# Attention, two MLPs and a Fourier stage in one kernel: a shorter conversion of doubles, and the state product in column halves

## The chip, the core and the metric

One NeuronCore of a Trainium2 chip runs the whole program in one launch. The metric is the device time of the launch in microseconds. Three timed executions of the kernel before gave 624.9, 626.17 and 627.99 us; the median is 626.17 us.

Engine names as in the profile: PE is the matrix engine (PEld its weight loads), DVE the VectorE, ACT the ScalarE, POOL the GpSimd, SP the queue from which nearly all transfers are issued.

## What is computed

Decayed linear attention over 2 batches and 8 heads, then a block that mixes tokens and channels, then a block with a two-dimensional Fourier transform, a normalisation and a channel MLP:

```python
for b in range(nb):                       # attention, block by block
    intra = einsum('bhic,bhjc->bhij', qb, kb) * Dmask
    intra = einsum('bhij,bhjd->bhid', intra, vb)
    inter = einsum('bhid,bhde->bhie', qb * lam_pow, kv_state)
    out[:, :, sl] = intra + inter
    kv_state = lam_block * kv_state + einsum('bhsd,bhse->bhde', kb * rev_pow, vb)
h = relu(xt @ w_tok1) @ w_tok2            # first block
u = x + h.transpose(0, 2, 1)
x = u + relu(u @ w_ch1) @ w_ch2
u = x + real(fft(fft(x, axis=1), axis=2)) # second block
out = u + relu(normalised(u) @ m_ch1) @ m_ch2
```

Sequence 768, head dimension 64, model dimension 512, hidden widths 256, 1536 and 2048, all results in float32. The weight matrices `w_tok1`, `w_tok2`, `w_ch1`, `w_ch2`, `m_ch1`, `m_ch2` reach the core as 64-bit floating point numbers, each read as two 32-bit words, and the core makes float32 of them itself.

## The kernel before, in words

**Attention** handles two heads at a time ("pairs", numbered 0 to 7, four for each batch), in six chunks of 128 positions. For each pair there are three steps. Scores (`s`, line 382): products of 64 rows, which DVE multiplies by the decay matrix (line 385). States (`u`, line 407): ACT first scales the keys (line 402), PE makes the chunk states, DVE chains them (lines 411 and 413). Result (`r`, `attention_out`, lines 417 to 434): ACT copies the states into a block-diagonal tile `bd` (line 424; first the states of two chunks, then of three), PE adds for each chunk the two heads' value products, each into its own 64 partitions (line 430), and from the second chunk on the state product (line 433), which takes both heads at once, 128 columns wide; ACT copies the result out after each three chunks (line 434). So there are 8 x 6 x 2 = 96 value products and 8 x 5 = 40 state products. The profile has two records for each of these float32 products.

**The order** of PE and SP is written out by hand. The string `EARLY` names the steps up to about 90 us in the order in which PE takes them (`s3` scores of pair 3, `u3` its states, `r3` its result, `x`, `h`, `o` the token mixing, `w` 8 idle transposes, `c` a turn of conversion, `l` a load, `m` a turn of the MLP). The order of DVE, ACT and POOL is set by the scheduler of the language, from the program's dependencies and its own costs. Each engine takes its instructions strictly in the order found so.

**Conversion.** A tile of doubles is loaded into a buffer `raw` (three of them; SP, line 185, waits until one is free). ACT takes the upper words into a tile `m` (`stage_abs`, line 204). DVE makes the float32 from `m` and the raw words (`word_ops`, lines 223 to 227): clamp, shift left by 3 and mask, put in the top bits of the lower word, put in the top bits of the upper word. The last of these frees the raw buffer. Then ACT rounds the tile (line 253) and POOL makes the remainder (line 254), and PE uses both in three products (lines 117 to 119). There are 63 conversions: 7 of token weights (tiles `m_t`), 56 of channel weights (`m_a`, `m_b`), 51 of them before 260 us and 12 between 440 and 540 us. In between weights come back from a scratch memory as float32.

**The rest**: from 90 us on PE runs the channel MLPs, with relu on ACT (line 486) and the remainder on DVE (line 487), the Fourier stage beside the MLP (260 to 440 us), and the last MLP in a form with seven instead of eight products (from 440 us on).

Of the kernel before, what the change touches and what calls it, by code (L numbers as in the profile page):

```python
# [14 lines left out]
AF = mybir.ActivationFunctionType  # L15
ALU = mybir.AluOpType
# [3 lines left out]
B, H, S, D = 2, 8, 768, 64  # L20
# [27 lines left out]
AHEAD = (10, 35)  # L48
BUFS = {"raw": 3, "man": 3, "hid": 4, "half": 5, "t": 9}

HI_LEAST = float(np.array(0x38000000, np.uint32).view(np.float32))
HI_MOST = float(np.array(0x47EFFFFF, np.uint32).view(np.float32))


def f32(ap):
    return ap.bitcast(F32)
# [3 lines left out]
def body(ctx: ExitStack, tc: tile.TileContext, qkv, kT, lam, w_tok1, w_tok2,  # L60
         w_ch1, w_ch2, m_ch1, m_ch2, dft, dft_x, out, scratch, singles):
    nc = tc.nc
# [14 lines left out]
    ts = nc.vector.tensor_scalar  # L77
    stt = nc.vector.scalar_tensor_tensor
# [61 lines left out]
    def width(key):  # L140
        return HS if key[0] == "t2" else 512
# [46 lines left out]
    def words(job):  # L188
        w = raws[job][:, :2 * width(job[1])].rearrange("p (n t) -> p n t", t=2)
        return w[:, :, 0], w[:, :, 1]  # L190

    def stage_abs():

        if at_["abs"] >= at_["load"]:
            return
        job = jobs[at_["abs"]]
        kind, key = job
        at_["abs"] += 1
        if kind in ("single", "sums"):
            return  # L200
        m = raw_p.tile([P, 512], U32, tag="man", name="m_" + "_".join(map(str, key)), bufs=BUFS["man"])[:, :width(key)]
        mans[job] = m
        with tc.issue_after(on_act["out", 1]):
            nc.scalar.activation(f32(m), f32(words(job)[1]), AF.Abs)  # L204

    def word_ops():


        job = jobs[at_["word"]]
        at_["word"] += 1  # L210
        if job[0] == "single":
            return []
        if job[0] == "sums":

            a11, a12, a21, a22 = (raws[job].bitcast(F32)[:, i * 256:(i + 1) * 256] for i in range(4))
            return [lambda: tt(out=a22, in0=a21, in1=a22, op=ALU.add),
                    lambda: tt(out=a21, in0=a11, in1=a21, op=ALU.subtract),
                    lambda: tt(out=a11, in0=a22, in1=a11, op=ALU.subtract),
                    lambda: tt(out=a12, in0=a12, in1=a11, op=ALU.subtract)]
        lo, hi = words(job)  # L220
        m = mans[job]
        del raws[job]
        return [lambda: ts(out=f32(m), in0=f32(m), scalar1=HI_LEAST, scalar2=HI_MOST, op0=ALU.max, op1=ALU.min),
                lambda: ts(out=m, in0=m, scalar1=3, scalar2=0x3FFFFFFF, op0=ALU.logical_shift_left,
                           op1=ALU.bitwise_and),
                lambda: stt(out=m, in0=lo, scalar=29, in1=m, op0=ALU.logical_shift_right, op1=ALU.bitwise_or),  # L226
                lambda: stt(out=m, in0=hi, scalar=0xC0000000, in1=m, op0=ALU.bitwise_and, op1=ALU.bitwise_or)]

    def stage_part():

# [30 lines left out]
    def convert(n=1, among=()):  # L261

        among = list(among)
        for _ in range(n):
            if at_["part"] < at_["word"] and (jobs[at_["part"]][0] == "ahead" or room(jobs[at_["part"]][1])):
                stage_part()
            if at_["word"] < at_["abs"] and at_["word"] < at_["part"] + 1:
                for op in word_ops():
                    op()
                    if among:  # L270
                        among.pop(0)()
            while at_["load"] < at_["word"] + BUFS["raw"] and len(raws) < BUFS["raw"] and load_next():
                pass
            if at_["abs"] < at_["word"] + 1:
                stage_abs()
        for op in among:
            op()
# [139 lines left out]
    def attention_out(b, hp, bd, bank):  # L417
        n = f"{b}_{hp}"
        t, sts, state = pair.pop((b, hp))
        v, qs = (t[:, i, :].rearrange("p (c j) -> p c j", j=C) for i in (2, 3))  # L420
        for cs in (slice(0, 2), slice(2, NC - 1)):
            for a in range(2):
                r = slice(a * D, (a + 1) * D)
                on_act["state", NP * b + hp] = nc.scalar.activation(bd[r, cs, r], state[r, cs, :], AF.Copy).ins
        for g in range(2):
            po = bank(f"po_{n}_{g}")
            for c in range(3 * g, 3 * g + 3):
                cs = slice((c - 3 * g) * C, (c - 3 * g + 1) * C)
                for a in range(2):
                    nc.tensor.matmul(po[a * D:(a + 1) * D, cs], v[:, c, a * D:(a + 1) * D],  # L430
                                     sts[c, a], start=True, stop=(c == 0), skip_group_check=True)
                if c > 0:
                    nc.tensor.matmul(po[:, cs], bd[:, c - 1, :], qs[:, c, :], start=False, stop=True, skip_group_check=True)
            on_act["out", NP * b + hp] = nc.scalar.activation(xT[b][:, hp, g * HS:(g + 1) * HS], po[:, :HS], AF.Copy).ins


# [532 lines left out]
    with tc.manual_schedule(engines={ENG.SP, ENG.PE}):  # L969
# [20 lines left out]
        def result(n):  # L990
            attention_out(n // NP, n % NP, bds[n % 2], x_bank if n == 7 else acc_bank)
# [155 lines left out]
```

## Time and profile before

| | us |
|---|---|
| timed executions, median (lowest to highest) | 626.17 (624.9 to 627.99) |
| the profiled execution, span of the core | 630.9 |
| PE busy in it | 605.1 (96%) |
| DVE busy | 459.5 (73%) |
| ACT busy | 236.2 (37%) |
| POOL busy | 145.2 (23%) |
| mean granted clock of PE | 0.985 |

Of the profiled execution only the span is given, not a time of its own by the clock of the timed ones. Its span is 4.7 us above the median of the timed executions. The busy time of an engine is the union of its records; a record of PE reaches to the modelled end of a product, so records overlap and the pace of PE is read from the starts.

### The profile page before, as it was taken

How to read it: one execution, taken by the hardware profiler on the slowest of the kernel's cores; microseconds unless marked ns; L12 is line 12 of the kernel's file. 1: busy time of each engine (PE TensorE's matmuls, PEld its weight loads, DVE VectorE, ACT ScalarE, POOL GpSimd, SP SyncE). 2: the span in 40 equal slices, each digit the busy share in tenths (PEclk: the TensorE clock that was granted, in tenths of full speed). 3: DMA queues.
4: the chain of work that ended last, by engine and by line, in shares of the span. 5: the costliest groups of instructions: out<-in, count | busy, mean ns of one | idle time of the engine just before them, and what ended most of it. 6: DMA issues, size and time to landing. Idle time of an engine off the chain costs nothing. (4 is left out here: it accounts for less than half of the span.)

```text
span 630.9 us, 9533 instructions
## 1 busy us (share of the span) xinstructions
PE 605.1 (96%) x3624; PEld 552.5 (88%) x3624; DVE 459.5 (73%) x886; ACT 236.2 (37%) x480; POOL 145.2 (23%) x119
## 2 busy tenths in 40 slices
PE   8899899989989999999999999999899998999997
PEld 7677689989988999999999999888799897889986
DVE  6698689999598838947696885785697798353535
ACT  2566454543233333233544451333353342311110
POOL 5153222312230040110262410024412242300000
PEclk9999799999999999999999999999999999999999
DMA  7953423425257727400032101002303524000005
GB/s 287 406 211 116 175 68 101 139 67 189 97 166 218 246 87 234 151 1 1 26 93 84 24 12 35 17 1 84 101 33 116 168 67 134 2 0 1 0 1 199
DMA packets 24637, 65.57 MB, mean 104 GB/s; under 512 B 2824, under 2 KB 3984, under 8 KB 24592
## 3 DMA queue, kind: packets, MB, share of 16 engines
q1 hardware_dynamic: 24304, 64.83, 30.8%
q8 instruction: 28, 0.46, 0.3%
q14 instruction: 17, 0.14, 0.1%
q10 hardware_dynamic: 288, 0.14, 0.1%
HBM read 54.99 MB, written 9.97 MB: 103 GB/s over the span
## 5 line engine op out<-in xcount | busy, mean ns | idle before, releaser
L119 PE MATMUL ac<-w_b,hid 128*128 128x512 f32 x192 | 75.9, 395 | 0.3 <-DVE hid L487 0.3
L118 PE MATMUL ac<-w_b,hid 128*128 128x512 f32 x192 | 75.7, 394 | 0.0
L117 PE MATMUL ac<-w_b,hid 128*128 128x512 f32 x192 | 74.9, 390 | 0.0
L487 DVE SCALAR_TENSOR_TENSOR hid<-ph,hid 128x384 fp32r<-128x384 f32 x68 | 37.6, 553 | 42.3 <-ACT hid L486 42.3
L118 PE MATMUL ac<-hid,w_b 128*128 128x384 f32 x192 | 65.0, 338 | 2.5 <-DVE hid L487 2.3
L117 PE MATMUL ac<-hid,w_b 128*128 128x384 f32 x192 | 64.8, 338 | 2.1 <-DVE xT L495 1.8
L119 PE MATMUL ph<-uh,w_a 128*128 128x384 f32 x192 | 64.3, 335 | 0.5 <-POOL w_a L254 0.5
L117 PE MATMUL ph<-uh,w_a 128*128 128x384 f32 x192 | 64.6, 337 | 0.0
L119 PE MATMUL ac<-hid,w_b 128*128 128x384 f32 x192 | 64.3, 335 | 0.0
L118 PE MATMUL ph<-uh,w_a 128*128 128x384 f32 x192 | 64.2, 334 | 0.0
L486 ACT ACTIVATE hid<-ph 128x384 fp32r<-128x384 f32 x68 | 33.0, 486 | 73.1 <-PE ph L119 72.9
L254 POOL TENSOR_TENSOR w_a<-m_a,w_a 128x512 fp32r<-128x512 f32 x18 | 25.8, 1434 | 105.2 <-ACT w_a L253 103.9
L119 PEld LDWEIGHTS ac<-w_b,hid 128*128 128x128 f32 x192 | 36.0, 188 | 8.5 <-DVE hid L487 0.8
L118 PEld LDWEIGHTS ac<-w_b,hid 128*128 128x128 f32 x192 | 36.0, 188 | 6.1
L117 PEld LDWEIGHTS ac<-w_b,hid 128*128 128x128 f32 x192 | 36.1, 188 | 5.8
L254 POOL TENSOR_TENSOR w_b<-m_b,w_b 128x512 fp32r<-128x512 f32 x18 | 25.6, 1420 | 67.7 <-ACT w_b L253 38.2
L118 PEld LDWEIGHTS ac<-hid,w_b 128*128 128x128 f32 x192 | 36.1, 188 | 4.5 <-DVE hid L487 4.5
L117 PEld LDWEIGHTS ac<-hid,w_b 128*128 128x128 f32 x192 | 36.1, 188 | 3.1 <-ACT m_b L204 1.3
L119 PEld LDWEIGHTS ph<-uh,w_a 128*128 128x128 f32 x192 | 36.0, 188 | 0.8 <-POOL w_a L254 0.8
L118 PEld LDWEIGHTS ph<-uh,w_a 128*128 128x128 f32 x192 | 36.1, 188 | 0.1
L117 PEld LDWEIGHTS ph<-uh,w_a 128*128 128x128 f32 x192 | 36.1, 188 | 0.1
L119 PEld LDWEIGHTS ac<-hid,w_b 128*128 128x128 f32 x192 | 36.1, 188 | 0.0
(456 smaller groups left out, 1499.9 us busy)
## 6 DMA issues: line engine op xcount, KB each, us to landing
qkv<-qkv SPq DMA_DIRECT2D x7, 768.0 KB, 8.4
single_scratch<-m_a SPq DMA_DIRECT2D x16, 256.0 KB, 4.2
qkv<-qkv SPq DMA_DIRECT2D x10, 384.0 KB, 5.7
kp<-kT SPq DMA_DIRECT2D x8, 384.0 KB, 6.6
out<-u SPq DMA_DIRECT2D x11, 256.0 KB, 2.0
single_scratch<-m_b SPq DMA_DIRECT2D x10, 256.0 KB, 4.3
raw_t_0d<-w_tok SPq DMA_DIRECT2D x2, 384.0 KB, 7.0
raw_t_1d<-w_tok SPq DMA_DIRECT2D x2, 384.0 KB, 3.2
```

What stands on the lines that cost most here:

```text
L117: nc.tensor.matmul(ps, wt[0], xt[0], start=first, stop=False, **kw)
L118: nc.tensor.matmul(ps, wt[0], xt[1], start=False, stop=False, **kw)
L119: nc.tensor.matmul(ps, wt[1], xt[0], start=False, stop=last, **kw)
L254: nc.gpsimd.tensor_tensor(out=t[:, 1, :n], in0=src, in1=f32(t[:, 0, :n]), op=ALU.subtract)
L486: nc.scalar.activation(hi, ps, AF.Relu)
L487: stt(out=lo, in0=ps, scalar=0.0, in1=f32(hi), op0=ALU.max, op1=ALU.subtract)
```

## The change

The clamp of the upper word is gone, so a conversion takes three DVE operations. ACT multiplies the upper words by 2 to the power -112 where it took their absolute value; DVE then shifts left by 3 (without a mask), puts in the lower word's bits, and puts in the sign (one bit where it was two). In attention the state product is issued once for each head, 64 columns wide, where it was issued once for both. Between lines 54 and 223 a line of the kernel before has a number one higher in the changed kernel, between lines 225 and 433 one lower, and from line 434 on the same.

```diff
-HI_LEAST = float(np.array(0x38000000, np.uint32).view(np.float32))
-HI_MOST = float(np.array(0x47EFFFFF, np.uint32).view(np.float32))
+DOWN = 2.0 ** -112
...
-            nc.scalar.activation(f32(m), f32(words(job)[1]), AF.Abs)
+            nc.scalar.activation(f32(m), f32(words(job)[1]), AF.Copy, scale=DOWN)
...
-        return [lambda: ts(out=f32(m), in0=f32(m), scalar1=HI_LEAST, scalar2=HI_MOST, op0=ALU.max, op1=ALU.min),
-                lambda: ts(out=m, in0=m, scalar1=3, scalar2=0x3FFFFFFF, op0=ALU.logical_shift_left,
-                           op1=ALU.bitwise_and),
+        return [lambda: ts(out=m, in0=m, scalar1=3, scalar2=None, op0=ALU.logical_shift_left),
                 lambda: stt(out=m, in0=lo, scalar=29, in1=m, op0=ALU.logical_shift_right, op1=ALU.bitwise_or),
-                lambda: stt(out=m, in0=hi, scalar=0xC0000000, in1=m, op0=ALU.bitwise_and, op1=ALU.bitwise_or)]
+                lambda: stt(out=m, in0=hi, scalar=0x80000000, in1=m, op0=ALU.bitwise_and, op1=ALU.bitwise_or)]
...
-                if c > 0:
-                    nc.tensor.matmul(po[:, cs], bd[:, c - 1, :], qs[:, c, :], start=False, stop=True, skip_group_check=True)
+                for a in range(2 if c > 0 else 0):
+                    nc.tensor.matmul(po[a * D:(a + 1) * D, cs], bd[:, c - 1, a * D:(a + 1) * D],
+                                     qs[:, c, :], start=False, stop=True, skip_group_check=True)
```

The scheduler of the language moves instructions of DVE and ACT with it; PE and SP keep their order, except for the doubled product. Three places:

PE, the second and third chunk of pair 0's result (`po` is the accumulator, `att` holds `bd`), before:

```order
L433 MATMUL po_0_0_289<-qkv_0_105,att 128x128
L430 MATMUL po_0_0_289<-st_0_0_213,qkv_0_105 64x128
L430 MATMUL po_0_0_289<-st_0_1_215,qkv_0_105 64x128
L433 MATMUL po_0_0_289<-qkv_0_105,att 128x128
L430 MATMUL po_0_1_299<-st_0_0_213,qkv_0_105 64x128
```

and now:

```order
L432 MATMUL po_0_0_289<-qkv_0_105,att 64x128 x2
L429 MATMUL po_0_0_289<-st_0_0_213,qkv_0_105 64x128
L429 MATMUL po_0_0_289<-st_0_1_215,qkv_0_105 64x128
L432 MATMUL po_0_0_289<-qkv_0_105,att 64x128 x2
L429 MATMUL po_0_1_301<-st_0_0_213,qkv_0_105 64x128
```

Every product of the step now has the shape 64x128; nothing else moves on PE.

DVE, around the scores of pair 6 (`st`) and the conversion of the token weights (`m_t_0_0` first, then `m_t_1_0`; `x_1` is the token mixing's input), before:

```order
L223 TENSOR_SCALAR m_t_0_0_718<-m_t_0_0_718 128x384
L224 TENSOR_SCALAR m_t_0_0_718<-m_t_0_0_718 128x384
L385 TENSOR_TENSOR st_2_0_648<-s_2_0_0_638,att 128x512
L385 TENSOR_TENSOR st_2_1_650<-s_2_0_1_639,att 128x512
L385 TENSOR_TENSOR st_1_2_637<-s_2_1_0_652,att 128x256
L385 TENSOR_TENSOR st_1_2_637<-s_2_1_1_653,att 128x256
L113 TENSOR_TENSOR x_1_661<-px_3_662,x_1_661 128x512
L113 TENSOR_TENSOR x_1_661<-px_4_669,x_1_661 128x512
L113 TENSOR_TENSOR x_1_661<-px_5_676,x_1_661 128x512
L226 SCALAR_TENSOR_TENSOR m_t_0_0_718<-raw_t_0_0d,m_t_0_0_718 128x384
L223 TENSOR_SCALAR m_t_1_0_735<-m_t_1_0_735 128x384
L227 SCALAR_TENSOR_TENSOR m_t_0_0_718<-raw_t_0_0d,m_t_0_0_718 128x384
```

and now:

```order
L224 TENSOR_SCALAR m_t_0_0_740<-m_t_0_0_740 128x384
L225 SCALAR_TENSOR_TENSOR m_t_0_0_740<-raw_t_0_0d,m_t_0_0_740 128x384
L226 SCALAR_TENSOR_TENSOR m_t_0_0_740<-raw_t_0_0d,m_t_0_0_740 128x384
L224 TENSOR_SCALAR m_t_1_0_756<-m_t_1_0_756 128x384
L384 TENSOR_TENSOR st_2_0_673<-s_2_0_0_663,att 128x512
L384 TENSOR_TENSOR st_2_1_675<-s_2_0_1_664,att 128x512
L384 TENSOR_TENSOR st_1_2_662<-s_2_1_0_677,att 128x256
L384 TENSOR_TENSOR st_1_2_662<-s_2_1_1_678,att 128x256
L225 SCALAR_TENSOR_TENSOR m_t_1_0_756<-raw_t_1_0d,m_t_1_0_756 128x384
L114 TENSOR_TENSOR x_1_686<-px_3_687,x_1_686 128x512
L114 TENSOR_TENSOR x_1_686<-px_4_694,x_1_686 128x512
L114 TENSOR_TENSOR x_1_686<-px_5_701,x_1_686 128x512
```

The last operation on `m_t_0_0`, which frees its raw buffer, has moved from behind seven operations on scores and inputs to before them.

ACT, around the states of pairs 6 and 7 (`qkv_3` is pair 7's tile, `state_2` pair 6's states, `xT` the results), before:

```order
L486 ACTIVATE h1s_1_0_802<-h_0_1_783 128x512
L253 ACTIVATE w_a_0_997<-m_a_0_984 128x512
L424 ACTIVATE att<-state_2_823 64x2x64
L402 ACTIVATE qkv_3_807<-qkv_3_807,att 128x5x64 x2
L424 ACTIVATE att<-state_2_823 64x2x64
L424 ACTIVATE att<-state_2_823 64x3x64 x2
L204 ACTIVATE m_b_0_995<-raw_b_0d 128x512
L204 ACTIVATE m_a_1_1006<-raw_a_1d 128x512
L434 ACTIVATE xT_178<-po_2_0_876 128x384
```

and now:

```order
L401 ACTIVATE qkv_3_832<-qkv_3_832,att 128x5x64
L486 ACTIVATE h1s_1_0_827<-h_0_1_808 128x512
L401 ACTIVATE qkv_3_832<-qkv_3_832,att 128x5x64
L205 ACTIVATE m_b_0_1027<-raw_b_0d 128x512
L423 ACTIVATE att<-state_2_848 64x2x64 x2
L205 ACTIVATE m_a_1_1037<-raw_a_1d 128x512
L423 ACTIVATE att<-state_2_848 64x3x64 x2
L205 ACTIVATE m_b_1_1062<-raw_b_1d 128x512
L434 ACTIVATE xT_178<-po_2_0_901 128x384
```

The first steps of three conversions (`m_b_0`, `m_a_1`, `m_b_1`) now stand ahead of pair 6's state copies and of its first result copy; before, two of them stood between these.

## Rows read from the trace of the kernel before

**Rows 1.** The page, engines: busy time, share of the span, instructions.
```profile
PE 605.1 (96%) x3624; PEld 552.5 (88%) x3624; DVE 459.5 (73%) x886; ACT 236.2 (37%) x480; POOL 145.2 (23%) x119
```

**Rows 2.** Stretches: length, busy PE, PEld, DVE, ACT, POOL, then PE's clock, DMA.
```profile
100.00:260.00 160.00, 153.10 (x851) 147.74 (x851) 130.85 (x231) 56.80 (x105) 32.88 (x24) 1.00 0.50 160
...
440.00:540.00 100.00, 95.33 (x465) 85.25 (x464) 82.43 (x150) 38.58 (x72) 29.17 (x20) 0.98 0.30 98
```

**Rows 3.** One stretch of PE alone: length, busy, clock, DMA share, GB/s.
```profile
69.80:80.00 10.20, 10.20 (x47) 0.50 0.15 53
```

**Rows 4.** Waits of PE's weight loads, whole span: us in total, times, longest.
```profile
PEld po L433 <- issue: 7.6, 39, 0.3
...
PEld ac L118 <- DVE hid L487: 4.5, 7, 1.6
PEld pc L117 <- DVE hid L487: 3.8, 2, 3.1
PEld ht L117 <- DVE xT L477: 2.5, 2, 1.8
```

**Rows 5.** Timeline of PE, result of pair 0: start us, length us, records.
```profile
12.19 0.66 PE L430 MATMUL po<-st,qkv 128*64 128x128 f32 x8
12.78 0.49 PE L433 MATMUL po<-qkv,att 128*128 128x128 f32 x2
13.20 0.44 PE L430 MATMUL po<-st,qkv 128*64 128x128 f32 x4
13.56 0.49 PE L433 MATMUL po<-qkv,att 128*128 128x128 f32 x2
13.98 0.44 PE L430 MATMUL po<-st,qkv 128*64 128x128 f32 x4
```

**Rows 6.** Weight loads of lines 430 and 433: ns least, median, most.
```profile
L430 PEld LDWEIGHTS po<-st,qkv x192: 132/136/231, 12.2 to 85.9; 128*64 128x64 f32 x192
...
L433 PEld LDWEIGHTS po<-qkv,att x80: 186/189/338, 12.8 to 86.3; 128*128 128x128 f32 x80
```

**Rows 7.** Timeline of PE, result of pair 6.
```profile
74.07 0.70 PE L430 MATMUL po<-st,qkv 128*64 128x128 f32 x4
...
75.42 0.70 PE L430 MATMUL po<-st,qkv 128*64 128x128 f32 x4
```

**Rows 8.** Timeline of PE: the states of pairs 2, 3 and 7.
```profile
19.77 1.19 PE L407 MATMUL u<-qkv 128*64 128x64 f32 x19 [0.82 <-ACT qkv L402]
...
28.20 1.12 PE L407 MATMUL u<-qkv 128*64 128x64 f32 x11 [1.63 <-ACT qkv L402]
...
68.64 1.19 PE L407 MATMUL u<-qkv 128*64 128x64 f32 x19 [1.85 <-ACT qkv L402]
```

**Rows 9.** Timeline of ACT: a conversion's first step, the keys of pair 4.
```profile
27.03 0.66 ACT L204 ACTIVATE m_t<-raw_t_0d 128x512 f32<-128x512 f32 x1 [1.48 <-DMA raw_t_0d<-w_tok]
...
33.48 1.01 ACT L402 ACTIVATE qkv<-qkv,att 128x320 f32<-128x320 f32 x2 [3.19 <-DMA qkv<-qkv]
```

**Rows 10.** Timeline of SP's transfer issues: two token weights; pair 7's keys and values.
```profile
41.72 14.41 SPq L185 DMA_DIRECT2D raw_t_1d<-w_tok  x2
...
58.87 0.43 SPq L362 DMA_DIRECT2D qkv<-qkv  x1
```

**Rows 11.** Waits of SP's queue, whole span: total, times, longest.
```profile
SPq L185 <- DVE m_t L227: 20.1, 5, 13.6
```

**Rows 12.** Line 223 by stretch: length, DVE busy, clock, DMA share, GB/s.
```profile
100.00:260.00 160.00, 18.96 (x37) 1.00 0.50 160
440.00:540.00 100.00, 4.94 (x12) 0.98 0.30 98
```

**Rows 13.** The chain of waits, 444 to 456 us: start us, us, what.
```profile
445.51 3.19 DMA raw_a_10d<-m_ch
...
449.42 0.44 DVE m_a L223
```

**Rows 14.** ACT: line 204 in one conversion; a scaled copy of 256 columns (ns).
```profile
L204 ACT ACTIVATE m_a<-raw_a_0d x1: 671/671/671, 61.6 to 61.6; 128x512 f32<-128x512 f32 x1
...
L766 ACT ACTIVATE y_1s<-y x4: 400/412/423, 295.0 to 366.1; 128x257 f32<-128x257 f32 x2, 128x255 f32<-128x255 f32 x2
```

## The prediction

> **What bounds the kernel now.** I read the table of engines first: PE is busy for 605.1 of 630.9 us, DVE for 459.5, ACT for 236.2 [rows 1]. So the end comes earlier only where PE has less to do, waits less, or runs at a better clock; work taken from DVE or ACT counts through these alone. Then the stretches, for the change works in three of them. From 100 to 260 us PE is busy for 153.10 of 160 us and DVE for 130.85; from 440 to 540 us PE for 95.33 of 100, DVE for 82.43 [rows 2]. The first 90 us hold the attention, and there the clock is the third matter: from 69.8 to 80.0 us PE is never idle and runs at 0.50, its lower level of 1.2 GHz [rows 3]. The waits of the weight loads then tell for whom PE waits [rows 4]: for DVE's `hid` in the MLPs (4.5 us in seven waits, 3.8 in two), and 39 times, 7.6 us in all and never over 0.3, in front of line 433, the state product, with nothing but "issue" behind it. The timeline shows what that is [rows 5].
>
> **State product in halves, on PE.** A chunk of a pair's result takes 13.98 − 13.20 = 0.78 us: 13.56 − 13.20 = 0.36 from the first of its four value records to the state product, then 13.98 − 13.56 = 0.42 for the state product's two records [rows 5]. Without state products in between, PE does eight value records in 12.78 − 12.19 = 0.59 us [rows 5]; against four in 0.36, the other four took 0.23. After the change all products of a chunk have the shape of these: two heads' value products and two heads' state products, eight records, 2 x 0.23 = 0.46 us, 0.32 less a chunk. Bounds: no gain, if the halves cost the 0.42 that the wide product costs; at best 0.42 − 0.23 + (0.36 − 0.23) = 0.32. I take the upper end, since the wide product is the only one of another shape and the four records behind it are slow as well (0.36). Five such chunks a pair, eight pairs: 40 x 0.32 = 12.8 us of PE at full clock. At half clock a chunk takes 75.42 − 74.07 = 1.35 [rows 7], and should take 2 x 0.46 = 0.92.
>
> How much reaches the end goes by who holds PE next:
> - Pairs 0 and 1: nothing. The states of pairs 2 and 3 start at 19.77 and 28.20, after waits of 0.82 and 1.63 us for ACT's scaled keys [rows 8], and before that ACT had waited for a transfer (`raw_t_0d`, until 27.03) [rows 9]. What PE saves it waits longer.
> - Pairs 2 and 3: ACT gets pair 4's keys only at 33.48, from a transfer [rows 9]. Pair 2's result runs around that time, pair 3's after it. Of 2 x 1.6 (five chunks x 0.32) I take 1.4, bounds 0 and 3.2.
> - Pairs 4 and 5: nothing of the kind stands behind them; 2 x 1.6 = 3.2.
> - The states of pair 7 wait 1.85 us at 68.64 [rows 8]. The keys and values come late: SP was held at line 185 for a free raw buffer, 13.6 us at the longest [rows 11], between the issues that begin at 41.72 and last 14.41 [rows 10], and so issues pair 7's at 58.87 only. The buffer is freed by line 227 of `m_t_0_0`, which now stands ahead of pair 6's scores and the inputs of the mixing on DVE: seven operations earlier, and one operation of its own less. I expect SP free 4 to 5 us sooner. That covers the 1.4 + 3.2 = 4.6 us by which PE comes sooner, and takes some 0.8 off the 1.85 (bounds −4.6, which is the transfer landing as late as now, and +1.85).
> - Pair 6 runs at half clock: five chunks x (1.35 − 0.92) = 2.15. ACT has three conversions' first steps (671 ns each [rows 14]) among its state copies now, where it had two; I allow 0.35 for that and take 1.8.
> - The spell at half clock goes on to 80.0, some 3.6 us beyond pair 6, which costs 1.8. With a shorter wait ahead of it it may end sooner: half, 0.9, between 0 and the 5.1 that a spell of 10.2 us costs as a whole [rows 3].
> - Pair 7: 1.6.
>
> Attention in all: 1.4 + 3.2 + 0.8 + 1.8 + 0.9 + 1.6 = 9.7 us.
>
> **Three operations instead of four, on DVE.** Line 223 takes 18.96 us in 37 operations from 100 to 260 us, and 4.94 in 12 from 440 to 540 [rows 12]. All of it is taken from DVE. The other three operations keep their tiles and widths, only constants change: nothing. PE can get back no more than it idles there: 160 − 153.10 = 6.9 us and 100 − 95.33 = 4.7 [rows 2]. In the first stretch the waits that I see are for `hid`, which DVE makes between conversions [rows 4]; with 18.96 us less ahead of it, most of them should go: 4 of 6.9, bounds 0 and 6.9. In the second the longest wait is one of 3.1 us [rows 4], at the end of a chain of a transfer of 3.19 us, ACT and line 223's 0.44 [rows 13]. Of that chain only the 0.44 goes, and the DVE work queued ahead; but a PE that idles less also loses less clock, 0.98 being the mean there [rows 2], which is 2 us of 100. I take 3 of 4.7 + 2, bounds 0.4 and 5. From 260 to 440 us nothing is converted: 0.
>
> **The scaled upper words, on ACT.** Line 204 reads every second word of 128x512 and takes 671 ns; a copy with a scale takes 412 for 257 columns [rows 14]. Per column that is 1.3 and 1.6 ns, so a scaled conversion of 512 could take 0.82 at worst; 63 x 0.15 = 9.5 us of an engine that is busy 37% of the span [rows 1]. I take no change, as the fixed part of a 257-column operation is shared by fewer columns; the cover is ACT's idle time. At the worst price it would show in attention, where three such steps stand ahead of pair 6's copy: 0.45 us.
>
> **The sum.** 9.7 + 4.0 + 3.0 = 16.7, so the profiled span goes from 630.9 to 614.2. It stands 4.7 above the median of the timed executions, about one spell of half clock. If the timed ones don't have that spell, the 0.8 and 0.9 and part of pair 6's gain are not there (some 2.7 us): 626.2 − 14.0 = 612.2; if they do, 609.5. I say 611; by the bounds of the large terms 605 to 616.
>
> **Rivals.**
> - *Transfers and ACT hold the attention.* The gain of pairs 2 to 5 is eaten by a longer wait for pair 7's keys (−4.6 in the bound above), and PE is at half clock behind it as before. Left: 1.8 + 1.6 + 7 = 10.4, less some of the DVE term: 616 to 619. For it: every early step waits for transfers [rows 8, 9]. Against: the freed buffer [rows 11].
> - *DVE's relief brings nothing.* PE is busy 96% in both stretches, and behind DVE may come ACT's rounding or the transfer of the chain [rows 13]. Then only attention counts: 9.7 less 0 to 1, 617.
> - *Slower: the halves' weight loads aren't hidden.* The 64-column load takes 136 ns in line 430, the 128-column one 189 [rows 6]. The change has four loads and four records of products a chunk where it had two and two. If each load had to wait for the product before it, four of 0.136 and four products of about 0.115 (0.23 / 2) make 1.0 us instead of 0.42: 40 x 0.58 = +23, of which the waits of pairs 0 and 1 hide about 4, and DVE's 7 come off: 638. It turns the sign once a chunk's state product costs some 0.2 us more than now. Against it: in the first chunk four loads of 136 ns, 0.54 in all, fit into 0.23 us for four records [rows 5, 6], so loads do run beside other loads or products where the halves alternate. The Trainium skill, "TensorE: Matmul & The Clock Gate", Part 3, Packing small matmuls, says that a weight load overlaps running products only when it goes to other row groups; here all products have the same 128 rows, so by it this rival would hold. The rows disagree.
> - *The scaled copy is no cheaper way:* at 0.15 us more each it delays what DVE waits for, and takes back a part of the 7 us of DVE's term: 614 to 616, inside the forecast.
>
> **How the numbers follow.** Forecast 0.62; attention held by transfers 0.18; DVE's relief empty 0.14; weight loads not hidden 0.03; 0.03 for what I don't see. The low end, 602, has the whole of attention's 12.8, the 5.1 of clock and most of both DVE bounds; the high end, 620, has both of the first two rivals in part. A measurement of this kernel can tell about 0.5%, 3.1 us: faster is below 623.0, slower above 629.3. Both of the first two rivals are still faster; only both at full together come to the middle: same 0.06. Slower 0.04.
>
> **What would show it.** Right: after the change a chunk of pair 0's result takes 0.46 us from one value product to the next chunk's, and the waits of line 432 named "issue" are gone; pair 7's keys and values are issued before 55 us, and its states wait under 1.2 us; PE's idle time is near 3 us from 100 to 260, and DVE's busy time there down by 19. Wrong: a chunk above 0.7 us (the halves aren't packed); a wait of over 4 us ahead of pair 7's states; DVE down by 19 and PE's idle time still 7 (PE waits for others there); line 205 above 0.75 us. A time above 620 needs at least two of these, and one above 629 the third rival.

## The result: 1.2% faster, about half of what was forecast

The changed kernel took 619.68 us (median of four executions, 618.34 to 622.71) against 626.75 for the kernel before: a ratio of 0.9876 with the interval 0.9844 to 0.9908, so 7.1 us less. A later comparison, six executions against fourteen, gave 619.14 against 627.76, ratio 0.9862 (0.9825 to 0.9900). The forecast was 611, 15 us less, with 620 as its upper end: the sign was right, the gain forecast was twice what came, and the bounds of the large terms, 605 to 616, do not hold it.

The engines and the stretches of the changed kernel's profile, whose span is 617.2 us, answer to [rows 1 to 3]:

```profile
PE 589.6 (96%) x3704; PEld 545.2 (88%) x3704; DVE 438.3 (71%) x823; ACT 235.0 (38%) x480; POOL 144.4 (23%) x119
```

```profile
69.80:80.00 10.20, 10.20 (x88) 9.59 (x87) 10.20 (x20) 6.27 (x14) 2.88 (x3) 1.00 0.31 102
100.00:260.00 160.00, 155.58 (x872) 150.47 (x871) 112.25 (x194) 53.69 (x101) 30.09 (x21) 1.00 0.48 152
440.00:540.00 100.00, 96.01 (x477) 85.93 (x477) 77.83 (x136) 37.33 (x70) 27.71 (x20) 1.00 0.29 90
```

PE is busy 15.5 us less, by the halves and by the three stretches of half clock in the profile before, some 17 us in all, that are missing. From 100 to 260 us DVE has 18.6 us less to do, and PE's idle time there has fallen from 6.9 to 4.4 us; from 440 to 540 from 4.7 to 4.0. No stretch at half clock is left in this execution.

The second and third chunk of pair 0's result, to be held against [rows 5], and the loads of the halves, against [rows 6]:

```profile
12.84 0.39 PE L429 MATMUL po<-st,qkv 128*64 128x128 f32 x4
13.06 0.39 PE L432 MATMUL po<-qkv,att 128*64 128x128 f32 x4
13.28 0.39 PE L429 MATMUL po<-st,qkv 128*64 128x128 f32 x4
```

```profile
L432 PEld LDWEIGHTS po<-qkv,att x160: 132/137/137, 12.6 to 74.8; 128*64 128x64 f32 x160
```

A chunk takes 13.28 − 12.84 = 0.44 us instead of 0.78. The eight loads of a chunk, 8 x 0.137 = 1.1 us, lie within these 0.44. So the halves do on PE what was forecast (0.46), 40 x 0.34 = 13.6 us in all. Record by record, the trace shows the two heads' products starting 0.007 us apart, and such a pair every 0.11 us; of the whole product the second record started 0.21 us after the first. Why the wide records come so slowly no run isolates: that they were the only ones of another shape, as the prediction had it, is not tested.

Three groups of PE's waits, as [rows 4], and below them the waits inside the later pairs, from PE's timeline:

```profile
PEld u L406 <- ACT qkv L401: 6.2, 9, 2.0
PEld ac L119 <- DVE hid L487: 5.5, 9, 1.1
...
PEld po L432 <- ACT att L423: 1.9, 4, 1.0
```

```profile
33.93 0.56 PE L432 MATMUL po<-qkv,att 128*64 128x128 f32 x3 [1.72 <-ACT att L423]
...
35.59 0.71 PE L432 MATMUL po<-qkv,att 128*64 128x128 f32 x3 [0.34 <-ACT att L423]
...
39.78 0.44 PE L449 MATMUL px<-ident,xT 128*128 128x128 f32 x2 [0.89 <-ACT xT L434]
...
63.16 0.74 PE L406 MATMUL u<-qkv 128*64 128x64 f32 x17 [0.60 <-ACT qkv L401]
...
66.39 0.71 PE L432 MATMUL po<-qkv,att 128*64 128x128 f32 x3 [0.74 <-ACT att L423]
```

The 39 small stops called "issue" in front of the state product are gone (one entry of 1.9 us for line 432 still has that name among the waits of the loads; it is the stop at 33.93). In their place PE waits for ACT: for pair 3's state copies (1.72 and 0.34 us), for the copy of pair 3's result (0.89), for pair 6's state copies (0.74). The wait ahead of pair 7's states has fallen to 0.60 us [rows 8].

### The profile page after: what moved, and what is told of

It reads as the page before. It is cut to its first block, busy times and chain, and to the rows that moved or that the text cites. A ratio compares the mean times of both kernels' runs of the same rounds, so it can differ in the third digit from the quotient of the medians.

```text
span 617.2 us, 9630 instructions
## 1 busy us (share of the span) xinstructions
PE 589.6 (96%) x3704; PEld 545.2 (88%) x3704; DVE 438.3 (71%) x823; ACT 235.0 (38%) x480; POOL 144.4 (23%) x119
```

## The experiments

Every verdict is a ratio to the kernel before on the same chip; the medians of before in the three comparisons were 627.48, 627.92 and 627.76 us.

### What the kernel before does from one execution to the next

> The kernel before once more, for the clock and the span of each of its timed executions. Theory (the profiled execution of before was not a typical one: its three stretches at half clock cost some 8 us, and the timed executions mostly lack them): most executions have a mean granted clock of 0.99 or more and a span of 622 to 626 us, two us under their time; a new profile has less than 8 us of PE at 0.5. Rival (the stretches belong to the kernel, and its timed executions have them all): every execution shows a clock near 0.985 and a span near 631. Ratio 1.00 for both.

The kernel was not edited. Ratio 1.0026 (0.9993 to 1.0059), 627.94 us. The mean clock of its twelve executions lay between 0.988 and 0.997, their spans between 623.2 and 632.2 us; of 23 further ones two had a clock of 1.000 and spans of 621.9 and 623.3. The new profile has 625.5 us at a clock of 0.993, with two stretches of half clock, some 7 us. The theory holds in the main: eight of the twelve have a clock of 0.99 or more, though only six a span of 622 to 626 us. What the clock takes changes from one execution to the next, and the one that the prediction was worked from, with a clock of 0.985 and 630.9 us, is near the slow end of them. The time is some 1.8 us above the span throughout.

### One part at a time

The halves alone:

```diff
-                if c > 0:
-                    nc.tensor.matmul(po[:, cs], bd[:, c - 1, :], qs[:, c, :], start=False, stop=True, skip_group_check=True)
+                for a in range(2 if c > 0 else 0):
+                    nc.tensor.matmul(po[a * D:(a + 1) * D, cs], bd[:, c - 1, a * D:(a + 1) * D],
+                                     qs[:, c, :], start=False, stop=True, skip_group_check=True)
```

> The kernel before with the state product in halves and nothing else. Theory (most of the 7 us come from the halves: 40 chunks x 0.34 = 13.6 us of PE, of which some 9 go into waits for ACT and transfers): 4 to 6 us faster than before, 620.5 to 622.5. Rival (the halves alone gain next to nothing, since pair 7's keys come as late as before, and it is the freed raw buffer that lets the gain through): 0 to 2 us faster, and the wait ahead of pair 7's states grows to 4 us or more.

The shorter conversion alone (the changed kernel with the old state product; the diff above the other way round):

> The kernel before with the shorter conversion and nothing else. Theory (PE's waits behind 100 us come from single DVE operations in front of hid, of which few go): 1 to 3 us faster than before, 623.5 to 625.5, with DVE some 20 us less busy. Rival (the step that failed is the transfer of the gain in attention, and DVE's relief is worth the 7 us that were forecast): 5 to 8 us faster, 618.5 to 621.5.

The halves alone: 628.94 us, 1.0031 (1.0007 to 1.0055), no gain at all. The conversion alone: 619.37 us, 0.9875 (0.9845 to 0.9906), as much as the whole change. In both pairs the rival had the time. The first rival's reason did not come true, though: with the halves alone the wait ahead of pair 7's states is 2.29 us, not 4 or more (1.97 in the second trace of the kernel before), and pair 7's values are issued at 55.68 us (56.67 there).

The halves do arrive in attention. Where one and the same product starts was read from both traces, that of the kernel before at 625.5 us and that of the halves alone at 624.8: behind attention 86.39 against 81.25 us, 5.1 earlier with the halves; in the middle of the first MLP 128.91 against 126.81, 2.1 earlier; at its end 255.22 against 254.31, 0.9; the last one 0.6. The first of these products, before and with the halves:

```profile
86.39 0.34 PE L118 MATMUL ht<-w_t,h1s 128*128 128x384 f32 x1
```

```profile
81.25 0.34 PE L118 MATMUL ht<-w_t,h1s 128*128 128x384 f32 x1
```

The clock has a part in this: some 2 of the 5.1 are a stretch at half clock that only the first trace has in attention (0.98 up to 100 us), and 1.8 of what is given back is one that only the second has behind it (0.97 in the second row below). The rest, some 2.5 us, came back as idle time of PE: 8.9 us from 80 to 260 us, against 6.4 without the halves. The waits listed there grew from 3.9 to 5.4 us for DVE's `hid`, and from 0.8 to 3.1 for steps of ACT. These are single executions. Two of the changed kernel, at the same clock up to 450 us, lie 1.0 us apart behind attention and 1.8 at the end of the first MLP, so a smaller difference between traces carries little. The kernel with the halves alone, by stretch:

```profile
80.00:100.00 20.00, 19.43 (x116) 18.30 (x115) 19.90 (x33) 10.80 (x20) 7.10 (x5) 1.00 0.34 116
100.00:160.00 60.00, 57.01 (x307) 54.77 (x306) 51.59 (x89) 22.80 (x43) 13.44 (x10) 0.97 0.36 120
```

DVE is busy for 19.90 of 20 us where PE comes out of attention. It has the conversions of the MLP's weights to do there as well as the remainders that PE waits for. A full DVE alone does not show that PE waits for it: with the conversion alone it is as full in these 20 us, and PE is never idle.

```profile
80.00:100.00 20.00, 20.00 (x120) 19.30 (x119) 19.97 (x30) 11.10 (x21) 6.69 (x5) 1.00 0.36 117
```

That it is DVE that takes the gain is shown by the runs below, which change its work.

### Is it DVE's load, or the buffer that it frees earlier?

```diff
-                lambda: stt(out=m, in0=hi, scalar=0x80000000, in1=m, op0=ALU.bitwise_and, op1=ALU.bitwise_or)]
+                lambda: stt(out=m, in0=hi, scalar=0x80000000, in1=m, op0=ALU.bitwise_and, op1=ALU.bitwise_or),
+                lambda: ts(out=f32(m), in0=f32(m), scalar1=-3.0e38, scalar2=3.0e38, op0=ALU.max, op1=ALU.min)]
```

> The changed kernel with a fourth DVE operation a conversion, a clamp that changes nothing, put behind the one that frees the raw buffer. DVE has the load of before, the raw buffer is freed one operation earlier than before. Theory (the load is what counts): as the halves alone with the old conversion, 627 to 629.5, and PE waits for DVE behind 100 us as there. Rival (the earlier free buffer, hence the earlier transfers, is what counts): as the changed kernel, 619 to 621.

629.66 us, 1.0031 (1.0007 to 1.0055): the same as the halves with the old conversion, and 10 us above the changed kernel. Freeing the buffer one operation earlier, with DVE's load as before, brings nothing. It does not price an earlier transfer: pair 7's values are issued at 57.09 us in this trace, no earlier than in the kernel before (56.67). The trailing clamp also makes each conversion as long as before, not only DVE's load, and the scheduler orders DVE and ACT anew in every run here; no run holds these apart. That the load is what counts is read from the waits of PE. Those of its loads for a converted weight come to 1.2 us in all; the long ones are for what DVE makes besides (`hid` and `xT` for the MLPs, `u`, a sum in the last MLP) and, in attention, for ACT's keys:

```profile
PEld ac L119 <- DVE hid L488: 6.6, 7, 1.6
PEld u L407 <- ACT qkv L402: 5.5, 7, 2.2
PEld pb L118 <- DVE u L632: 4.7, 3, 3.3
PEld ht L118 <- DVE xT L478: 3.1, 4, 1.8
PEld pc L118 <- DVE hid L488: 3.0, 1, 3.0
```

Against the changed kernel's trace the same products start 2.8 us later behind attention (91.92 against 89.09), 5.8 at the end of the first MLP (264.24 against 258.41), 10.5 behind the last conversions (536.60 against 526.09). The clock has a large part: this trace has stretches of half clock from 19.4, 67.2 and 521.2 us, each 3.4 us long and so worth 1.7, that the changed kernel's has not. Without them nothing is left of the 2.8 beside attention, about 3 us are lost in the first MLP and about 3 behind 440 us. The next two runs take the places apart by the timed executions, with the trailing clamp in the conversions of one place only:

> The changed kernel once more, as the reference of the next three on one chip: 618.5 to 620.5 by every theory.

> The changed kernel with the trailing clamp in the twelve conversions behind 440 us alone. Theory (with the clamp in all conversions the trace fell back by 2.8 us up to 90 us, by 3.0 from there to 260, by 4.7 from 430 to 530; each stretch pays for its own operations): 3 to 5 us slower than the changed kernel, 622.5 to 624.5. Rival (the late loss came with the earlier ones, since the stretch was entered later): within 1 us of it.

> The changed kernel with the trailing clamp in the first sixteen conversions alone, those beside the attention. Theory (each stretch pays for its own): 2 to 3.5 us slower than the changed kernel, 621.5 to 623. Rival (what is lost in attention is got back behind it, where PE waits for DVE in any case): within 1 us of it.

```diff
+                lambda: ts(out=f32(m), in0=f32(m), scalar1=-3.0e38, scalar2=3.0e38, op0=ALU.max, op1=ALU.min)][:4 if job[0] == "double" and job[1][1] == 1 and job[1][0] in "ab" else 3]
```

(the late ones; for the early ones the condition is `at_["word"] <= 16`). The reference took 619.14 us (0.9862, 0.9825 to 0.9900); the late twelve 622.42 (0.9913, 0.9883 to 0.9944), 3.3 more; the first sixteen 621.84 (0.9906, 0.9869 to 0.9942), 2.7 more. Both are what the theory said, though the intervals overlap that of the reference. The first sixteen lie between 30 and 102 us of their trace. If the places add, some 4 of the 10 us are left for the 35 in between. Not all of this is waiting. With the product of span and mean clock taken as the span without the clock's losses, the means are 615.2 us (reference), 616.2 and 616.3: about 1 us each, within the scatter of the executions, and the rest goes with the mean clock, 0.9963 against 0.9927 and 0.9942.

### Still fewer operations

```diff
-                lambda: stt(out=m, in0=lo, scalar=29, in1=m, op0=ALU.logical_shift_right, op1=ALU.bitwise_or),
```

> The changed kernel without the operation that puts in the lower word's bits (the lowest three bits of each converted weight are left out): two DVE operations a conversion. Theory (DVE's load sets the pace behind the attention, so that what attention saves is given back there; the first operation taken away let it through, a second gives less): 2 to 4 us faster than the changed kernel, about 616. Rival (three operations are already off the path, PE's waits that are left are single operations in front of hid): within 1 us of the changed kernel, 619 to 620.5.

and without the shift as well:

> The changed kernel with one DVE operation a conversion, the sign (shift and lower word's bits left out, so the weights are wrong by a power of two and in their lowest bits). Theory (load): 1 to 2 us below the kernel with two operations, 614 to 615. Rival: as the changed kernel, 619 to 620.5.

Two operations: 615.43 us, 0.9797 (0.9763 to 0.9831), another 4 us. One: 616.91 us, 0.9823 (0.9793 to 0.9853), no further gain. The first of these kernels, by stretch:

```profile
80.00:100.00 20.00, 20.00 (x120) 19.19 (x119) 13.18 (x25) 10.15 (x20) 3.90 (x3) 1.00 0.40 135
100.00:160.00 60.00, 59.37 (x332) 57.39 (x331) 33.15 (x61) 21.31 (x41) 12.28 (x9) 1.00 0.27 92
```

With DVE at 46 of 80 us PE idles for 0.6 us in these, and little is left to relieve. But most of the 4 us are not won there, for the changed kernel idles for only 1.3 us in them. In the two traces the same products start within 0.2 us of each other at 440 us and 3.3 apart at 540, and from 440 to 540 us PE is busy for 98.55 us instead of 96.01. (Before that the trace with two operations loses 1.7 us by a stretch of half clock in attention, which the other has not.)

If that is the reason why the halves bring nothing, they should bring something here. So the state product was made whole again in the kernel with two operations (the first diff the other way round):

> The state product whole again, with two DVE operations a conversion (the lower word's bits left out, as in the run with two operations, which took 615.4 us with the halves). Theory (what the halves save in PE is given back to DVE as long as DVE has three or four operations; with two the halves pay): 3 to 5 us slower than with the halves, 618.5 to 620.5. Rival (the halves pay nothing whatever DVE does, because inside the attention ACT and transfers hold PE): 614.5 to 616.5.

618.66 us, 0.9847 (0.9812 to 0.9883), 3.2 us more than with the halves, as the theory had it; the two intervals overlap a little. In the two traces the halves are 3.6 us ahead behind attention (89.02 against 92.66) and still 2.8 at the end. All together, medians in us:

| DVE operations a conversion | state product whole | in halves |
|---|---|---|
| four | 626.8 to 627.9 | 628.9 (old conversion), 629.7 (trailing clamp) |
| three | 619.4 | 619.1 and 619.7 (the change) |
| two (lowest bits left out) | 618.7 | 615.4 |

### The waits for ACT inside attention

In the changed kernel ACT's timeline ahead of the waits at 33.93 and 35.59 us reads:

```profile
31.68 1.02 ACT L401 ACTIVATE qkv<-qkv,att 128x320 f32<-128x320 f32 x2 [3.12 <-DMA qkv<-qkv]
32.60 0.47 ACT L434 ACTIVATE xT<-po 128x384 f32<-128x384 f32 x1
32.97 0.61 ACT L252 ACTIVATE w_t<-m_t 128x512 fp32r<-128x512 f32 x1
33.49 0.62 ACT L423 ACTIVATE att<-state 64x128 f32<-64x128 f32 x2
```

Pair 4's keys, which wait for a transfer, stand ahead of pair 3's state copies. They were put behind them:

```diff
-        behind = (("table", 0), ("state", 0), ("out", 0), ("out", 1))[min(NP * b + hp, 3)]
+        behind = (("table", 0), ("state", 0), ("out", 0), ("out", 1), ("state", 3))[min(NP * b + hp, 4)]
```

> The changed kernel with one order on ACT altered: the scaling of pair 4's keys, which waits for a transfer, comes behind the copies of pair 3's states instead of ahead of them. Theory (the waits of 1.7 and 0.3 us of PE in pair 3's result, at 33.9 and 35.6 us of the changed kernel's trace, are this order's, and what they cost reaches the end): 1.5 to 2.5 us faster than the changed kernel, 617 to 618.5. Rival (the next wait takes it: the copies of pair 3's result, pair 5's keys or the inputs of the mixing come no earlier): within 0.7 us of the changed kernel, 619 to 620.5, and the waits stand a little later, in front of the mixing's inputs.

and in a second kernel the rounding of the first token weights too:

```diff
-        nc.scalar.activation(t[:, 0, :n], src, AF.Copy)
+        with tc.issue_after(on_act[("state", 3) if key[0] == "t1" else ("out", 1)]):
+            nc.scalar.activation(t[:, 0, :n], src, AF.Copy)
```

> The kernel with pair 3's state copies ahead of pair 4's keys, and in addition the rounding of the three first token weights on ACT (and with it POOL's remainder) behind those copies. Theory (the second copy of pair 3's states waited for DVE's chain, whose neighbours took 1.6 to 1.8 us instead of 0.7 while POOL made the remainder): PE's wait of 1.8 us in pair 3's result falls under 0.5, and the kernel is 1 to 2.5 us faster than 618.55, 616 to 617.5. Rival (the remainders then collide with what follows, the inputs of the mixing, whose wait grows by as much): 618 to 619.5.

618.55 us, 0.9863 (0.9829 to 0.9898), and 618.79, 0.9866 (0.9827 to 0.9905): not to be told from the change. The waits moved. PE's timelines of the first and of the second:

```profile
36.29 0.71 PE L432 MATMUL po<-qkv,att 128*64 128x128 f32 x3 [1.77 <-ACT att L423]
41.29 0.66 PE L449 MATMUL px<-ident,xT 128*128 128x128 f32 x4 [1.54 <-ACT xT L434]
```

```profile
33.93 0.71 PE L433 MATMUL po<-qkv,att 128*64 128x128 f32 x3 [0.59 <-ACT att L424]
39.30 0.77 PE L450 MATMUL px<-ident,xT 128*128 128x128 f32 x5 [2.62 <-ACT xT L435]
```

In the first the second state copy comes behind a rounding on ACT that waits 2.48 us for DVE:

```profile
35.35 0.63 ACT L252 ACTIVATE w_t<-m_t 128x512 fp32r<-128x512 f32 x1 [2.48 <-DVE m_t L226]
```

In the second the wait inside pair 3 is down to 0.59 us, close to what its theory said (under 0.5), and 2.62 stand in front of the mixing's inputs, as its rival said. No order tried here beats the change; the run with two operations does, but its weights lack their lowest three bits.

## Why the forecast was half right

**What held.** The chunk: 0.44 us for 0.46. Pairs 0 and 1 gain little: the states of pairs 1, 2 and 3 wait 1.79, 0.81 and 1.04 us in the changed kernel, and pair 3's start at 26.43 us, against 27.12 and 28.20 in the two traces of the kernel before. The wait ahead of pair 7's states is under 1.2 us, but the reason given, the buffer freed earlier, is not shown: its values are issued at 55.04 us (forecast: before 55), against 58.87 and 56.67 in the two traces of before and 55.68 with the halves and the old conversion. What goes with the wait is the conversion: it is 2.29 with the halves alone, 1.98 with the trailing clamp, and not there with the conversion alone. DVE's busy time from 100 to 260 us is down by 18.6 (forecast 19). ACT's scaled copy costs what the old step cost, 655 to 726 ns for a tile of 512.

**The step that failed is the transfer of attention's gain to the end**, in two ways.
- "Nothing of the kind stands behind them" (pairs 4 and 5, 3.2 us), and 1.4 and 1.8 for pairs 2, 3 and 6: the new waits for ACT add up to 1.72 + 0.34 + 0.89 + 0.74 = 3.7 us, at the very places where PE comes sooner; with the conversion alone no wait there is over 0.2. Pair 6's copies wait these 0.74 for DVE's chain of states, not for the conversions' first steps for which 0.35 were allowed; of the three only the first stands ahead of all of them. The traces with and without halves lie 3.6 to 3.9 us apart behind attention where their clocks are alike (two and three operations), not the 7.0 that the sum holds without the 2.7 that the prediction itself put to the clock's spell.
- The sum then carried what was left to the end. It does not keep: with four operations on DVE all of it was given back (5.1 us to 0.6 in the traces, the clock's part included, and nothing left in the times), with three more than half (3.9 to 1.5), with two little (3.6 to 2.8). In the times the halves are worth −1.5 us, about 0 and 3.2. The trace had part of this: DVE at 130.85 of 160 us [rows 2] is a mean, and in the first 60 of them it was busy for 56.42.

**The other term was sized about right and placed wrongly.** DVE's relief was put at 7 us behind attention and measured at 8 alone and 10 with the halves. But nothing was counted for the conversions beside attention, which are worth 2.7 in the times; the late twelve are worth 3.3 (forecast 3). PE's idle time fell less than forecast: to 4.4 us from 100 to 260, where 3 were expected, and from 4.7 to 4.0 in the late stretch. The rest there was to come from the clock, and one trace of the changed kernel has 1.00 from 440 to 540 us, the other 0.98, as before. The two terms were added, 9.7 + 7, as if each had its own share of the path. Alone they are worth 0 and 8, together 7 to 9.

**The reference.** The prediction knew that its profile stood 4.7 us above the median and took one stretch of half clock off; the trace has three, and the executions timed later run from 0.983 to 1.000 of full clock. By the product of span and mean clock, an estimate of the span without the clock's losses, the kernel before has 622.8 us (mean of 23), the halves 622.6, the conversion 617.1, the trailing clamp 621.4, the change 616.8 and 615.2 in its two comparisons (622.4 for the kernel before in the second): some 6 to 7 us are waits and work, the rest of the 7 to 8.6 is clock. The mean clock was 0.9947 before, 0.9993 with the conversion alone, 0.9922 with the halves alone; but 0.9943 and 0.9908 with two and one operations, so that fewer waits for DVE do not simply go with a better clock. What sets it, no run isolates.

**The rivals.** "Transfers and ACT hold the attention" had nearly the right time, 616 to 619 for 619.7 and 619.1, and half of the mechanism: ACT's state copies, not pair 7's keys. That its time came out is luck: it kept 3.4 us of attention's gain and 7 of DVE's, where the runs give about 0 and 8. "DVE's relief brings nothing" is refuted; with three operations it is all of the gain. The rival of the weight loads is refuted too, for they are hidden: 1.1 us of loads in a chunk of 0.44. The Trainium skill, "TensorE: Matmul & The Clock Gate", Part 3, says that a load overlaps running products only in other row groups; here all loads go to the same 128 rows, so the trace does not agree.

## What to carry to other kernels

Before a gain of an early stage is added to the sum, look at the engine that feeds the next stages, in short stretches and together with the waits for it: where it is nearly full, an earlier start can be given back, and what relieves that engine counts first. A full engine alone does not prove it. Two savings on different engines of one chain need not add; predict the pair, and test each alone and both. And read more than one execution of the kernel before, with its clock, before a profile's waits at half clock are counted as there to be won.

## What was not expected of the hardware

A DVE operation on two tiles (lines 225 and 226 of the changed kernel) takes 0.67 to 0.70 us for 512 columns, and 1.3 to 2.1 when POOL is at work as it begins, as here:

```profile
30.36 1.84 DVE L225 SCALAR_TENSOR_TENSOR m_t<-raw_t_1d,m_t 128x512 uint32<-128x512 uint32 x1
...
32.31 0.68 DVE L226 SCALAR_TENSOR_TENSOR m_t<-raw_t_1d,m_t 128x512 uint32<-128x512 uint32 x1
```

```profile
29.80 1.84 POOL L388 TENSOR_TENSOR qkv<-qkv,att 128x640 f32<-128x640 f32 x1 [6.12 <-DMA qkv<-qkv]
```

POOL's operation ends at 31.64; DVE's, begun at 30.36, ends 0.55 us after that. In the whole trace 21 of 118 such operations begin while POOL is at work; 20 of them are long, and each of these ends 0.55 us after POOL's does. The Trainium skill, "SBUF — State Buffer", SBUF: two separate sides, says that the two engines share a pair of ports, held by one of them for a whole instruction, and the trace agrees with that. A DVE operation taken away beside POOL's work can be worth more than it costs alone: line 223, of one tile, took 0.43 us at the median from 100 to 260 us, up to 1.52, and 0.51 on average (18.96 / 37) [rows 12].

One kernel's executions spread over 10 us (623.7 to 634.2) while the mean granted clock went from 1.000 to 0.987, which is some 8 of the 10 by the product of span and clock.
